# Output weights loaded between the two halves of a chunk's keys, and the keys of the last but one chunk in quarters

## The chip, the cores and the metric

One core of one Trainium2 chip runs the kernel; the rest of the chip is idle. The metric is device time in microseconds (us), the median of several executions.

## The reference, cut to what matters

Two decode attentions stand side by side. Part A has grouped heads and a window of 2048 positions; part B has 32 heads, 4 batches and the whole cache of 8192 positions. Part B is where the time is.

```
q = (x @ wq)                                # B = 4 rows, one token each
scores = einsum("bhqd,bhkd->bhqk", q, k_cache) * Dh ** -0.5     # 32 heads, Sk = 8192, Dh = 128
p = softmax(scores)
o = einsum("bhqk,bhkd->bhqd", p, v_cache)
out = o @ wo
```

Keys and values of part B are 537 MB of the 587 MB that have to be read, and each byte is used once. That is why loads are at the heart of it.

## The kernel before: the parts that matter

Part B is cut into 32 chunks (numbers 8 to 39) of 16 MB: four heads of one batch. A chunk has a stretch T on TensorE (PE), in which its keys are transposed and multiplied with q, then the statistics of the softmax, then the stretch PV with the values. Four chunks in a row (a group) share 512 KB of output weights, held in one buffer, `wos`. SyncE posts all big loads, in the order of the program, and waits before each until its buffer is free:

```
def dma_wos(hq):
    ...
    sch.add_dma("sp", <load B_wo of group hq into wos>, "d_wos",
                waits=[("reord", NCA + 4 * hq - 1)] if hq else [], ...)

for c in range(NCA, NC):            # NCA = 8, NC = 40
    if (c - NCA) % NB == 0:         # a new group
        dma_wos((c - NCA) // NB)
    dma_B("k", c)                   # two halves, 4 MB each; each waits for T of the half that it overwrites
    dma_B("v", c)                   # 8 MB; waits for PV of the chunk before
```

`reord` is the last PE instruction that reads the old output weights. It comes after all of T of the last chunk of a group. GpSimd relays the landings to PE: a first key half of a new group is called ready when both it and `wos` have landed.

The last chunks use smaller pieces, counted in tiles of 128 positions: keys of chunk 38 in `NEXTK = (64, 64, 128)`, values of 37 and 38 in `NEXTV = (128, 64, 64)`.

Of the kernel before, what the change touches and what calls it, by code (L numbers as in the profile page):

```python
# [13 lines left out]
TG = 8  # L14
# [6 lines left out]
SLAG = 2  # L21
NW = 64
LASTK = (32, 32, 64, 64, 64)
NEXTK = (64, 64, 128)
NEXTV = (128, 64, 64)
LASTV = (128, 64, 32, 16, 8, 8)
QK = (0, 4, 8, 16, 24)
QV = (0, 16, 24, 28, 30, 31)
# [140 lines left out]
def bass_concat_heads__sliding_block_cached__mha_block_cached__decode_kernel(  # L169
# [39 lines left out]
    NTA, NTB = chunks[0]["NT"], chunks[-1]["NT"]  # L209
    NONE = NC  # L210
    chunks.append(dict(chunks[NCA]))
    assert sum(LASTV) == sum(LASTK) == sum(NEXTK) == sum(NEXTV) == NTB and NTA * 16 == 1024 and NTB * 4 == 1024

    sch = _Sched()
    with ExitStack() as es:
        block = es.enter_context(nc.Block())

        def sb(name, shape, dt):
            return es.enter_context(nc.sbuf_tensor(name, shape, dt))
# [6 lines left out]
        wos = sb("wos", [P, 4, DO], BF16)  # L226
# [40 lines left out]
        semnames += ["d_h%d" % i for i in range(NH)] + ["d_bk0", "d_bk1", "d_bv0"]  # L267
        semnames += [f + str(i) for f, x in (("d_lk", LASTK), ("d_nk", NEXTK), ("d_lv", LASTV), ("d_nv", NEXTV)) for i in range(len(x))]
        semnames += ["d_wo%d" % i for i in range(NWO)] + ["d_wos"]
        sems = {n: es.enter_context(nc.semaphore(n)) for n in semnames}  # L270
# [43 lines left out]
        held = [[] for _ in range(NH)]  # L314
# [10 lines left out]
        def flat(at, n):  # L325
            return kv[:, at:at + n, :].rearrange("p s x -> p (s x)")
# [21 lines left out]
        def dma_wos(hq):  # L348


            src = B_wo[4 * hq * P:4 * (hq + 1) * P, :].rearrange("(p r) n -> p (r n)", r=4)
            sch.add_dma("sp", lambda e: e.dma_start(wos[:, :, :].rearrange("p r n -> p (r n)"), src), "d_wos",
                        waits=[("reord", NCA + 4 * hq - 1)] if hq else [], key=("wos", hq))
# [6 lines left out]
            src = T[:, ch["g"], SkA - W:, :].rearrange("b (pp j) d -> pp b (j d)", pp=P // NB)  # L360
            sch.add_dma("sp", lambda e: e.dma_start(kv[:, at, :], src), "d_h%d" % at, waits=waits, key=(kind, c))

        def dma_B(kind, c):


            ch = chunks[c]
            T, at, steps = (B_k, KB, QK) if kind == "k" else (B_v, VB, QV)
            src = T[ch["b"], 4 * ch["hq"]:4 * ch["hq"] + 4].rearrange("u (pp j) d -> (u pp) (j d)", pp=P // 4)
            dst = flat(at, 4)
            if kind == "k":  # L370
                pieces, fam = (LASTK, "d_lk") if c == NC - 1 else (NEXTK, "d_nk") if c == NC - 2 else ((NTB // 2,) * 2, "d_bk")
            else:
                pieces, fam = (LASTV, "d_lv") if c == NC - 1 else (NEXTV, "d_nv") if c in (NC - 2, NC - 3) else ((NTB,), "d_bv")
            j0, unit = 0, NTB // 4
            for i, n in enumerate(pieces):
                waits = []
                for u in range(j0 // unit, (j0 + n - 1) // unit + 1):
                    waits += held[at + u]
                x = slice(j0 * P, (j0 + n) * P)
                sch.add_dma("sp", lambda e, x=x: e.dma_start(dst[:, x], src[:, x]), fam + str(i), waits=waits, key=(kind, c, i))  # L380
                j0 += n
                sch.relay("pool", sems, "r_" + kind, n // TG, [(kind, c, i)] + ([("wos", ch["hq"])] if i == 0 and kind == "k" and ch["b"] == 0 else []))
            for g, end in zip(steps, steps[1:] + (NTB // TG,)):
                sch.tk[(kind + "r", c, g)] = ("r_" + kind, (c - NCA) * (NTB // TG) + end)
            for u in range(4):
                held[at + u] = [("T", ch["s"] + (u + 1) * unit // TG - 1) if kind == "k" else ("pv", c)]

        KB, VB = 0, 4

# [9 lines left out]
            dma_wo(c)  # L399
        for c in range(NCA, NC):  # L400
            if (c - NCA) % NB == 0:
                dma_wos((c - NCA) // NB)
            dma_B("k", c)
            dma_B("v", c)

        ms_read = []
# [495 lines left out]
```

## Time and profile before

| | before |
|---|---|
| median of the first three runs | 1386.8 us (1385.33 to 1389.99) |
| the profiled run | 1388.96 us, span 1387.2 us |
| DMA queue busy | 98.6% of 16 engines' span |
| PE busy | 89% |
| read from HBM | 587.21 MB, 423 GB/s over the span |

### The profile page before, as it was taken

The page shows a single profiled execution, that of the slowest core. Times are in us where ns is not written, and L with a number is a line of the kernel's source. Part 1 is how long each engine was busy: PE and PEld are TensorE (multiplying, and loading weights), DVE is VectorE, ACT ScalarE, POOL GpSimd, SP SyncE. Part 2 cuts the span into 40 slices and gives each one's busy share as a digit, 9 for nine tenths or more (in the row PEclk, how much of TensorE's full clock was granted, in tenths as well). Part 3 has the DMA queues.
Part 4 walks back from the last instruction along what each step waited for, and adds up shares of the span by engine and source line. Part 5 has one row for each costly group of instructions (what it writes and reads, how often), then busy time and mean ns, then how long its engine had stood idle before and what let it go on. Part 6 is the DMA issues. An engine that isn't in the chain of part 4 may idle for free.

```text
span 1387.2 us, 60816 instructions
## 1 busy us (share of the span) xinstructions
PE 1234.2 (89%) x27417; PEld 1137.9 (82%) x27417; DVE 744.6 (54%) x1335; ACT 513.9 (37%) x649; POOL 9.8 (1%) x29
## 2 busy tenths in 40 slices
PE   4898799989888989989898999989988889989998
PEld 4786788888887888888887888978888789878887
DVE  1675456655554556545554565545555555545555
ACT  1553244423333344333333443333333443333333
POOL 2000000000000000000000000000000000000000
PEclk9998999999999999999998899999999999999999
DMA  9999999899999999999999999999999999999997
GB/s 400 425 426 444 413 410 437 364 439 423 440 437 405 426 439 435 427 438 423 440 437 406 435 433 433 444 389 423 454 415 417 435 427 438 423 438 423 423 429 327
DMA packets 20652, 587.51 MB, mean 424 GB/s; under 512 B 2308, under 2 KB 2328, under 8 KB 4760
## 3 DMA queue, kind: packets, MB, share of 16 engines
q1 hardware_dynamic: 20600, 587.21, 98.6%
q8 instruction: 15, 0.25, 0.1%
q14 instruction: 5, 0.04, 0.0%
q10 hardware_dynamic: 32, 0.01, 0.0%
HBM read 587.21 MB, written 0.01 MB: 423 GB/s over the span
## 4 chain that ended last, share of the span: by engine, by line
DMA 55%; PE 41%; DVE 2%; issue 1%; ACT 1%; SPq 0%; POOLq 0%; DVEq 0%
DMA kv<-in_B_v_cache_dram 45%; PE po L414 20%; PE tr L412 12%; DMA kv<-in_B_k_cache_dram 8%; PE sc L414 6%; DMA kv<-in_B_wq_dram 2%; PE ms L414 1%; PE tr L414 1%; DMA kv<-in_A_k_cache_dram 1%; PE fin L414 1%; ACT pbb L594 1%; DVE kt L479 1%; DVE sA L532 0%; PE ms L412 0%; DVE gm L563 0%
## 5 line engine op out<-in xcount | busy, mean ns | idle before, releaser
L412 PE MATMUL tr<-identb,kv 128*128 128x128 bf16 x8704 | 666.7, 221 | 29.5 <-POOLq L72 23.3
L479 DVE COPY kt<-tr 128x1024 bf16<-128x1024 bf16 x736 | 501.9, 691 | 240.6 <-PE tr L412 238.0
L477 ACT ACTIVATE kt<-tr 128x1024 bf16<-128x1024 bf16 x352 | 359.6, 1024 | 730.8 <-PE tr L412 730.7
L412 PEld LDWEIGHTS tr<-identb,kv 128*128 128x128 bf16 x8704 | 508.9, 99 | 41.2 <-issue 31.0
L414 PE MATMUL sc<-qq,kt 128*128 128x64 bf16 x8192 | 398.0, 191 | 12.2 <-DVE kt L479 10.2
L414 PEld LDWEIGHTS po<-pbb,kv 128*128 128x128 bf16 x8192 | 306.2, 108 | 66.4 <-issue 56.4
L414 PE MATMUL po<-pbb,kv 128*128 128x64 bf16 x8192 | 309.8, 208 | 43.8 <-POOLq L72 39.6
L414 PEld LDWEIGHTS sc<-qq,kt 128*128 128x128 bf16 x8192 | 331.6, 98 | 15.7 <-DVE kt L479 13.1
L594 ACT ACTIVATE pbb<-sc,negb 32x128 bf16<-32x128 f32 x256 | 137.5, 537 | 123.2 <-DVE negb L577 120.1
L414 PE MATMUL tr<-wos,back 32*128 32x512 bf16 x512 | 80.5, 408 | 27.3 <-DVE kv L709 27.3
L661 DVE RECIPROCAL rinv<-ms 128x4 f32<-128x4 f32 (+1 forms) x40 | 7.8, 196 | 158.7 <-PE ms L414 158.7
L709 DVE CAST kv<-tr 128x512 bf16<-128x512 f32 x128 | 81.3, 683 | 12.3 <-PE tr L414 12.3
L599 DVE TENSOR_REDUCE rsb<-pbb 128x4 f32<-128x1024 bf16 x32 | 39.0, 1220 | 51.9 <-ACT pbb L594 51.9
L414 PEld LDWEIGHTS tr<-wos,back 32*128 32x128 bf16 x512 | 23.2, 96 | 49.1 <-DVE kv L709 30.1
L548 DVE TENSOR_REDUCE rh<-sc 128x4 f32<-128x512 f32 x64 | 43.9, 686 | 14.3 <-PE sc L414 14.3
L683 DVE TENSOR_TENSOR oz<-po,rz 128x16 bf16<-128x16 f32 x32 | 5.6, 175 | 67.9 <-PE po L414 67.9
L414 PE MATMUL sc<-qb,kt 128*128 128x64 bf16 (+3 forms) x512 | 26.4, 197 | 0.5 <-DVE gx L569 0.4
L414 PEld LDWEIGHTS ms<-gm,ind 4*128 4x128 f32 x64 | 9.4, 182 | 18.0 <-DVE gm L563 18.0
L414 PEld LDWEIGHTS sc<-qb,kt 128*128 128x128 bf16 x512 | 22.1, 102 | 2.4 <-issue 1.4
L414 PE MATMUL po<-pba,kv 128*128 128x64 bf16 x512 | 20.2, 198 | 3.1 <-issue 1.8
L414 PE MATMUL ms<-gm,ind 4*128 4x4 f32 x64 | 12.2, 258 | 11.9 <-DVE gm L563 11.9
L414 PEld LDWEIGHTS po<-pba,kv 128*128 128x128 bf16 x512 | 17.6, 101 | 5.1 <-ACT pba L616 4.2
(63 smaller groups left out, 210.7 us busy)
## 6 DMA issues: line engine op xcount, KB each, us to landing
kv<-in_B_k_cache_dram SPq DMA_DIRECT2D x61, 4096.0 KB, 26.4
kv<-in_A_k_cache_dram SPq DMA_DIRECT2D x8, 2048.0 KB, 13.3
kv<-in_A_v_cache_dram SPq DMA_DIRECT2D x8, 2048.0 KB, 14.6
kv<-in_B_v_cache_dram SPq DMA_DIRECT2D x3, 4096.0 KB, 21.4
kv<-in_B_v_cache_dram SPq DMA_DIRECT2D x5, 2048.0 KB, 27.5
kv<-in_B_k_cache_dram SPq DMA_DIRECT2D x5, 2048.0 KB, 28.4
kv<-in_A_wq_dram SPq DMA_DIRECT2D x1, 4096.0 KB, 12.5
kv<-in_B_wq_dram SPq DMA_DIRECT2D x1, 4096.0 KB, 27.1
```

The costliest lines, as they stand in the source:

```text
L412: sch.add("pe", lambda e: e.transpose(o, l, r), waits, key)
L414: sch.add("pe", lambda e: e.matmul(o, l, r, start=start, stop=stop), waits, key)
L477: sch.add("act", lambda e: e.activation(dst, src, ACTF.Copy), waits=waits, key=("ev", s))
L479: sch.add("dve", lambda e: e.tensor_copy(dst, src), waits=waits, key=("ev", s))
L548: sch.add("dve", lambda e: e.tensor_reduce(out=rh[:, half, :], in_=src, axis=AX.X, op=ALU.max), waits=[("S", ch["s"] + (half + 1) * ch["NG ...
L594: sch.add("act", lambda e, src=src, dst=dst, pp=pp, u=u: e.activation(dst, src, ACTF.Exp, bias=negb[pp, 0, u:u + 1], scale=scale), waits=[ ...
L599: sch.add("dve", lambda e: e.tensor_reduce(out=rst[1][:, :], in_=probs_of(c).rearrange("p j u -> p u j"), axis=AX.X, op=ALU.add), waits=[( ...
L661: sch.add("dve", lambda e: e.reciprocal(out=ri, in_=ms[:, L0:L0 + n]), waits=[("L", c)], key=("rinv", c))
L683: sch.add("dve", lambda e: e.tensor_tensor(out=o, in0=i0, in1=i1, op=ALU.mult), waits=waits, key=("oT", c))
L709: sch.add("dve", lambda e: e.tensor_copy(wol[:, u, :], o), waits=[("reord", c) if u == 3 else ("reord", c, u)] + [("fin", prev(c))], key=( ...
```

## The change

Its intent: the wait of the output weights should no longer hold up both halves of the next keys. The first half goes ahead of it. The diff, cut to its core (the rest lets one half be posted alone):

```
-NEXTK = (64, 64, 128)
-NEXTV = (128, 64, 64)
+NEXTK = (64, 64, 64, 64)
+NEXTV = (128, 64, 32, 32)
 ...
-    sch.relay("pool", sems, "r_" + kind, n // TG, [(kind, c, i)] + ([("wos", ch["hq"])] if i == 0 and kind == "k" and ch["b"] == 0 else []))
+    sch.relay("pool", sems, "r_" + kind, n // TG, [(kind, c, i)] + ([("wos", ch["hq"])] if i == 1 and kind == "k" and ch["b"] == 0 else []))
 ...
     if (c - NCA) % NB == 0:
+        dma_B("k", c, 0)
         dma_wos((c - NCA) // NB)
-    dma_B("k", c)
+        dma_B("k", c, 1)
+    else:
+        dma_B("k", c)
     dma_B("v", c)
```

More of the change, by code (lines that the diff above doesn't have):

```diff
@@ L361, in dma_A, with dma_B @@
             sch.add_dma("sp", lambda e: e.dma_start(kv[:, at, :], src), "d_h%d" % at, waits=waits, key=(kind, c))
-        def dma_B(kind, c):
+        def dma_B(kind, c, part=None):
             ch = chunks[c]
@@ L373, in dma_B @@
                 pieces, fam = (LASTV, "d_lv") if c == NC - 1 else (NEXTV, "d_nv") if c in (NC - 2, NC - 3) else ((NTB,), "d_bv")
-            j0, unit = 0, NTB // 4
+            j0, unit, used = 0, NTB // 4, {}
             for i, n in enumerate(pieces):
+                if part is not None and i != part:
+                    j0 += n
+                    continue
                 waits = []
@@ L378, in dma_B @@
                     waits += held[at + u]
+                    used[at + u] = [("T", ch["s"] + (u + 1) * unit // TG - 1) if kind == "k" else ("pv", c)]
                 x = slice(j0 * P, (j0 + n) * P)
@@ L381, in dma_B @@
                 j0 += n
-                sch.relay("pool", sems, "r_" + kind, n // TG, [(kind, c, i)] + ([("wos", ch["hq"])] if i == 0 and kind == "k" and ch["b"] == 0 else []))
+                sch.relay("pool", sems, "r_" + kind, n // TG, [(kind, c, i)] + ([("wos", ch["hq"])] if i == 1 and kind == "k" and ch["b"] == 0 else []))
             for g, end in zip(steps, steps[1:] + (NTB // TG,)):
                 sch.tk[(kind + "r", c, g)] = ("r_" + kind, (c - NCA) * (NTB // TG) + end)
-            for u in range(4):
-                held[at + u] = [("T", ch["s"] + (u + 1) * unit // TG - 1) if kind == "k" else ("pv", c)]
+            for u in used:
+                held[u] = used[u]
         KB, VB = 0, 4
```

## The prediction

> **What bounds the kernel now.** I read the page's busy shares first, then the chain of waits, the issue times of the DMA queue, and the DMA share in short windows. Names: c is a chunk, c = 0 to 7 in part A and 8 to 39 in part B; K0(c) and K1(c) are the two halves of its keys (4 MB each), V(c) its values (8 MB), wos the 512 KB of output weights that serve four chunks. T is the stretch of transposes and scores on PE, PV the stretch with the values.
>
> ```profile
> span 1387.2 us, 60816 instructions
> ...
> PE 1234.2 (89%) x27417; PEld 1137.9 (82%) x27417; DVE 744.6 (54%) x1335; ACT 513.9 (37%) x649; POOL 9.8 (1%) x29
> ...
> q1 hardware_dynamic: 20600, 587.21, 98.6%
> ...
> DMA 55%; PE 41%; DVE 2%; issue 1%; ACT 1%; SPq 0%; POOLq 0%; DVEq 0%
> ```
>
> PE at 89% looks like a candidate, but the DMA queue is busy 98.6% of the span. The chain in order of time says where each sets the pace:
>
> ```profile
> 284.75 31.96 DMA kv<-in_B_v_cache_dram
> ...
> 326.50 28.98 DMA kv<-in_B_v_cache_dram
> ...
> 364.71 29.55 DMA kv<-in_B_v_cache_dram
> ...
> 404.48 28.55 DMA kv<-in_B_v_cache_dram
> ...
> 442.70 31.62 DMA kv<-in_B_v_cache_dram
> ```
>
> Start plus duration is the landing of a V: 316.71, 355.48, 394.26, 433.03, 474.32. The steps are 38.77, 38.78, 38.77 and then 41.29. Inside a group of four chunks the step never leaves 38.8 by more than 0.5: that is 16 MB at full rate, and the DMA is the bound. Across a group boundary it is longer. Why, the DMA queue and short windows show at the first boundary (c = 11 to 12):
>
> ```profile
> 247.06 0.33 SPq L380 DMA_DIRECT2D kv<-in_B_v_cache_dram  x1
> 274.57 0.33 SPq L352 DMA_DIRECT2D wos<-in_B_wo_dram  x1
> 274.94 0.91 SPq L380 DMA_DIRECT2D kv<-in_B_k_cache_dram  x2
> 284.75 0.33 SPq L380 DMA_DIRECT2D kv<-in_B_v_cache_dram  x1
> 298.88 11.15 SPq L380 DMA_DIRECT2D kv<-in_B_k_cache_dram  x2
> ```
> ```profile
> 267.00:269.00 2.00, 2.00 (x52) 2.00 (x50) 1.33 (x3) 1.02 (x1) 0.00 (x0) 1.00 1.21 524
> 269.00:271.00 2.00, 1.70 (x30) 0.89 (x28) 1.37 (x3) 0.00 (x0) 0.00 (x0) 1.00 0.00 0
> 271.00:273.00 2.00, 0.78 (x4) 0.40 (x4) 1.31 (x4) 0.83 (x2) 0.00 (x0) 0.99 0.00 0
> 273.00:275.00 2.00, 2.00 (x14) 0.82 (x13) 1.34 (x3) 1.94 (x5) 0.00 (x0) 0.50 0.00 0
> 275.00:277.00 2.00, 2.00 (x42) 2.00 (x40) 0.68 (x2) 1.54 (x3) 0.00 (x0) 0.50 0.69 231
> ```
>
> The last two columns are DMA share and GB/s, counted where a packet starts (a window may read over 1 or 0 for that reason). No packet starts from 269 to 275. In an ordinary chunk (last line of the queue) K0 is posted when half of T is done and K1 11.15 us later. At a boundary nothing is posted between 247.06 and 274.57, because wos stands ahead of both and waits for the last reorder matmul of the chunk before, which comes after all of T. The table of the queue's waits has it: 7 waits, 189 us.
>
> ```profile
> SPq L352 <- PE tr L414: 189.0, 7, 27.3
> ```
>
> **What the Trainium skill says.** "DMA: Bandwidth & Descriptors", Anatomy of one DMA: DMA engines do not wait on semaphores; the issuing sequencer waits before it dispatches. So one blocked issue holds everything behind it, as the trace shows above. Same page, Queues, rings and completion order: on each engine descriptors are taken in ring order; a K0 posted early thus queues behind V and takes nothing from it. The trace agrees: K0 posted at 298.88 landed at 326.43, 9.72 after V. "HBM Reference", Specifications, gives about 425 GB/s for one core alone; the page here has a mean of 424, so there is no rate to be won, only idle time. "TensorE: Matmul & The Clock Gate", What's actually happening: PE falls to half clock after some 3.4 us of idleness. The windows show 0.50 near boundaries, so a PE that waits is slow just after; this shortens if the wait goes, and is no gain of its own while DMA is the bound.
>
> **The change part by part.** (1) K0 goes ahead of wos; wos then stands between K0 and K1, and the signal that K1 is ready, not K0, carries wos. No bytes and no compute instructions are added. Per boundary the cost now is the V-to-V step minus what a full queue would need: 38.78 for keys and values plus 1.22 for wos (512 KB loads behind other loads land 1.21 to 1.23 apart in part A). From the landings in the trace the seven steps are 45.28, 41.28, 40.51, 41.98, 41.35, 41.37 and 41.02: sum 292.79. Less 7 x 40.00 leaves 12.79 us: 5.28 at the first, 0.5 to 2.0 at each of the six others, where wos is posted only about 1 us ahead of V's landing, too late to start without a gap.
>
> Does the queue stay full afterwards? First boundary: T of c = 11 starts at 247.03, half of it is done after 10.9 us, so K0(12) is posted near 258, while V(11) moves until 271. K0 covers until 280.7. wos and K1 are posted at 274.6 to 275.4 as now, 5 us in hand. They last until 291.6, and V(12) is posted at 284.75. At the other boundaries the reorder ends about 1 us before V lands, so nearly all of K0's 9.7 us is in hand. So I take back all 12.79.
>
> (2) Keys of c = 38 in four quarters instead of 64, 64, 128. The chain at the end reads as if a load of 26.71 us set the pace, but the PE line shows what PE really waited:
>
> ```profile
> 1294.59 26.71 DMA kv<-in_B_k_cache_dram
> ```
> ```profile
> 1321.39 0.62 PE L412 MATMUL tr<-identb,kv 128*128 128x128 bf16 x8 [0.69 <-POOLq L72]
> ```
>
> T of c = 38 has run since 1309.5 on the first half; it stopped for 0.69 us before the big piece landed at 1321.29. In quarters the third lands some 4.85 earlier (1316.4), the fourth at 1321.4, when PE needs it only at about 1326. So 0.69 us is saved, not 4.85. From the landing of V(36) (1262.87) on PE is never idle longer than that: PV 9.5, then cycles of 36.7 (the PVs start at 1300.16, 1337.76, 1374.49). The end is a PE chain of 124 us hung on V(36); it moves with V(36) as a whole. Packets of half size cost the DMA, by the packet records, 9.78 instead of 9.70 us for the keys and 0.12 us for each of the two V tails. The last V landed at 1380.14 while PV ended at 1383.9, so this fits in the slack.
>
> (3) V tails of c = 37 and 38 in 32, 32 instead of 64: no gain. V(38) had landed at 1340.80, and PV needed its last quarter at 1344.4.
>
> Sum: 12.8 + 0.7 = 13.5 us. 1386.8 - 13.5 = 1373.3 us, a ratio of 0.990.
>
> **The rivals.** PE takes over as the bound. For: PV starts of c = 9 to 11 are 198.83, 236.66 and 274.54, steps of 37.8, only 1 us under the DMA's 38.78, and the chain there is PE's. With V(12) landing at 311.4, PE could start PV(12) only near 274.54 + 37.7 = 312.2: it gives back 0.8 at once. Against: the DMA doesn't starve from that (V(13) is posted at 322, K1(13) ends at 331), and PE regains 1 us per chunk. If the 0.8 stayed lost to the end, 1374.
>
> The wait moves to K1. If wos were released later than K0 ends, each boundary would run dry again. For: K1 is now posted about 5 us later than in an ordinary chunk. Against: the 5 to 9 us in hand worked out above. If half the gain were lost, 1380.
>
> The quarters give the full 4.85. For: the chain gives the big load 26.71 us. Against: the 0.69 of idle PE. It would be 1369.
>
> Nothing comes of it because the end is PE's: 1386. Against: the PE chain starts from a landing, and that moves.
>
> **Range and chances.** The runs of before spread from 1385.33 to 1389.99. With that and the rivals, 1370 to 1378 should hold it 8 times in 10. Two per cent faster would be 1359; all DMA idle time in the middle is 12.8, so this is out of reach: 0.02. Nothing is added that could cost 27 us: 0.01. Within 2%: 0.97.
>
> **What would show it.** Right: DMA share near 1 in every window from 247 to 1370; V-to-V steps at all seven boundaries near 40.0; V(36) landing near 1250; K0 at boundaries posted about half a T before wos; the 0.69 us wait of PE in c = 38 gone; PVs at the end still 36.7 apart. Wrong: windows of zero share behind a boundary's K0 (the wait moved to K1), V-to-V steps still above 41 at boundaries, or a chain that is PE's throughout part B.

## More of the kernel before

The page's second part cuts the span into 40 slices of 34.7 us. Its last row is what the DMA engines moved in each, in GB/s:

```profile
GB/s 400 425 426 444 413 410 437 364 439 423 440 437 405 426 439 435 427 438 423 440 437 406 435 433 433 444 389 423 454 415 417 435 427 438 423 438 423 423 429 327
```

Most slices are near 430. The eighth, 364, covers 243 to 277 us, where the first boundary between two groups of part B lies; slice 27 with 389 covers the boundary at 905 us. Such a row finds a hole quickly, but doesn't measure it: packets count where they start.

## The result, and the profile after

| | before | after |
|---|---|---|
| median | 1388.1 us (1385.33 to 1392.59, 6 runs) | 1374.87 us (1374.67 to 1377.15, 6 runs) |
| span of the profiled run | 1387.2 us | 1373.0 us |
| DMA queue busy | 98.6% | 99.5% |

The ratio is 0.9906, with a 95% interval of 0.9887 to 0.9925. Here and below a ratio is the mean time of one kernel's fast runs over that of the other's fast runs of the same rounds, so it isn't quite the ratio of the medians. The predicted ratio was 0.990, the predicted time 1373.3. All outputs are right.

Lines of the page of the changed kernel, for the ones that the prediction and the last section showed:

```profile
span 1373.0 us, 60822 instructions
...
GB/s 401 425 427 443 422 422 435 432 431 436 437 432 428 431 432 432 434 438 435 433 432 420 433 435 430 437 439 430 428 430 432 431 435 439 433 428 430 422 428 319
...
q1 hardware_dynamic: 21032, 587.21, 99.5%
...
DMA 52%; PE 43%; DVE 2%; ACT 1%; issue 1%; SPq 0%; POOLq 0%; ACTq 0%; DVEq 0%
```

Between the head and the last slice no slice is under 420. The issues of SyncE at the first boundary (start, duration, what) and the short windows there (PE, weight loads, DVE, ACT, GpSimd, then PE's clock, DMA share, GB/s):

```profile
243.38 0.33 SPq L384 DMA_DIRECT2D kv<-in_B_v_cache_dram  x1
254.27 0.33 SPq L384 DMA_DIRECT2D kv<-in_B_k_cache_dram  x1
270.98 0.33 SPq L352 DMA_DIRECT2D wos<-in_B_wo_dram  x1
271.35 0.43 SPq L384 DMA_DIRECT2D kv<-in_B_k_cache_dram  x1
280.87 0.33 SPq L384 DMA_DIRECT2D kv<-in_B_v_cache_dram  x1
```
```profile
269.00:271.00 2.00, 1.94 (x7) 0.55 (x8) 1.22 (x4) 1.95 (x4) 0.00 (x0) 0.50 1.03 442
271.00:273.00 2.00, 2.00 (x40) 2.00 (x40) 0.81 (x2) 1.80 (x4) 0.00 (x0) 0.50 0.99 426
273.00:275.00 2.00, 2.00 (x42) 2.00 (x40) 1.09 (x1) 0.00 (x0) 0.00 (x0) 0.50 0.95 410
```

The first half of the keys is now posted at 254.27, 10.89 us behind V. The output weights still wait until 270.98, but the DMA engines have the half to work on: a share of 1 where there was 0. The wait itself hasn't gone away, as the table of the queue's waits shows. It was 189.0 us before; what is left no longer holds up a load that the DMA engines run short of:

```profile
SPq L352 <- PE tr L421: 111.8, 7, 16.4
```

**Where the 14.26 us between the two profiled runs come from.** I followed the landings of V, as in the prediction. V of chunk 36 landed 14.24 us earlier (1262.87, then 1248.63); from there to the end both take the same, 124.37 and 124.33. The 14.24 split so: the seven boundary steps sum to 280.39 instead of 292.79 (each is now 40.05 or 40.06), which is 12.40. The 21 other steps sum to 1.50 less: 39.64, 39.01 and 39.22 at chunks 9, 17 and 22 became 38.8. V of chunk 8 landed 0.36 earlier. That is 14.26, the 0.02 too much being rounding. So 12.40 of it are where they were predicted. Two things were not: the 1.9 us away from the boundaries, and the tail, which gained nothing although it should have gained 0.7.

### The profile page after: what moved, and what is told of

It is laid out like the page before. It is cut to its first block, busy times and chain, and to the rows that moved or that the text cites. A ratio compares the mean times of both kernels' runs of the same rounds, so it can differ in the third digit from the quotient of the medians.

```text
span 1373.0 us, 60822 instructions
## 1 busy us (share of the span) xinstructions
PE 1229.9 (90%) x27417; PEld 1134.6 (83%) x27417; DVE 744.4 (54%) x1335; ACT 513.3 (37%) x649; POOL 9.8 (1%) x29
## 3 DMA queue, kind: packets, MB, share of 16 engines
q1 hardware_dynamic: 21032, 587.21, 99.5%
## 4 chain that ended last, share of the span: by engine, by line
DMA 52%; PE 43%; DVE 2%; ACT 1%; issue 1%; SPq 0%; POOLq 0%; ACTq 0%; DVEq 0%
DMA kv<-in_B_v_cache_dram 47%; PE po L421 22%; PE tr L419 12%; PE sc L421 6%; DMA kv<-in_B_k_cache_dram 2%; DMA kv<-in_B_wq_dram 2%; PE ms L421 1%; PE tr L421 1%; ACT pbb L601 1%; DMA kv<-in_A_k_cache_dram 1%; PE fin L421 1%; DVE sA L539 1%; DVE kt L486 1%; PE ms L419 0%; DVE gm L570 0%
## 6 DMA issues: line engine op xcount, KB each, us to landing
kv<-in_A_wq_dram SPq DMA_DIRECT2D x1, 4096.0 KB, 12.4
```

## The experiments

Theory A: the wait at the head of SyncE's queue emptied the DMA engines, and the gain is that idle time. Its rivals: B, that PE was sped up because first halves are now called ready without the output weights; C, that the quartered keys bring a large part; D, that it matters that the weights travel behind a half. All twelve kernels were timed in five rounds. For the first four the kernel before had a median of 1386.39 us, for the second four 1386.32, for the last four 1387.61.

| run | median us | ratio to before | 95% interval |
|---|---|---|---|
| move alone | 1376.12 | 0.9926 | 0.9912 to 0.9940 |
| pieces alone | 1385.45 | 0.9994 | 0.9977 to 1.0012 |
| weights posted by GpSimd | 1376.51 | 0.9926 | 0.9912 to 0.9940 |
| move, but not in the first group | 1376.92 | 0.9933 | 0.9919 to 0.9948 |
| first group alone | 1386.34 | 0.9996 | 0.9978 to 1.0014 |
| moved, but ready late | 1376.67 | 0.9931 | 0.9914 to 0.9947 |
| an eighth ahead | 1379.56 | 0.9952 | 0.9936 to 0.9968 |
| more loads in pieces | 1373.70 | 0.9908 | 0.9893 to 0.9922 |
| the changed kernel again | 1375.64 | 0.9916 | 0.9902 to 0.9929 |
| the move alone again | 1376.34 | 0.9919 | 0.9906 to 0.9931 |
| more loads in pieces again | 1374.81 | 0.9907 | 0.9893 to 0.9922 |
| weights behind both halves | 1376.80 | 0.9921 | 0.9907 to 0.9934 |

One thing holds for all variants that free half or all of the keys: the boundary steps came out as theory A expected, and where a gain in us was expected, it came out smaller. For the move alone 12.8 to 14 us were expected, for GpSimd's queue 12 to 13, for ready late about 12.4; the ratios give 9.6 to 11.2. The traces say why: V of chunk 36 landed at 1262.87, 1256.58 and 1258.11 in the three kept traces with the old order, 1259.2 in the mean, and at 1248.6 to 1249.5 in the eight that free half or all of the keys (those with more loads in pieces left out), 1248.9 in the mean. That is 10.3 us. The expectations had been taken from the first trace alone, the latest of the three.

### The move alone, and the pieces alone

```
# move alone: the changed kernel with
 NEXTK = (64, 64, 128);  NEXTV = (128, 64, 64)
# pieces alone: the kernel before with
 NEXTK = (64, 64, 64, 64);  NEXTV = (128, 64, 32, 32)
```

> Only the output weights move between the two key halves; keys of the last but one chunk and the value tails stay as before. Theory A (the blocked issue of the output weights emptied the DMA queue): the whole gain but for the last-chunk part, 12.8 to 14 us, ratio 0.990; the step from one landing of V to the next is 40.0 at all seven boundaries; PE's 0.69 us wait in chunk 38 is back. Theory C (the quartered keys bring a large part, up to 4.9 us): only 8 to 9 us, ratio 0.994.

> Only the quartered keys and the finer value tails; the output weights stand ahead of the keys as before. Theory A: 0.0 to 0.7 us, ratio 0.9995 to 1.000, V-to-V steps of 41 to 45 at the boundaries as before, PE's wait in chunk 38 gone. Theory C: 4 to 5 us, ratio 0.9965.

The move alone takes 1376.12 us, 10.3 us under before; the boundary steps in its trace are 40.05 to 40.08, and the wait of 0.69 us in chunk 38 is back, as expected. By its time alone it would not decide: 0.9926 lies between what A (0.990) and C (0.994) expected. The pieces alone do. They are not to be told from before, and the 0.9965 that C expected lies outside their interval. C falls.

The pieces-alone trace held a surprise. It has the old order, but its boundary steps sum to 286.77, not 292.79: the idle time there is 6.4 us over 7 x 40.06 and not 12.4. In the first step alone, 43.15 stands against 45.28. I come back to this below.

### The weights from another queue

```
-sch.add_dma("sp", lambda e: e.dma_start(wos[...], src), "d_wos", ...
+sch.add_dma("pool" if hq else "sp", lambda e: e.dma_start(wos[...], src), "d_wop" if hq else "d_wos", ...
-... if i == 0 and kind == "k" ...
+... if i == 1 and kind == "k" ...
```

> The output weights keep their place ahead of both key halves in time, but are posted by GpSimd instead of SyncE, so that their wait blocks nobody's keys; both key halves of a boundary are then posted at half and at all of T as in other chunks; the first group's stay on SyncE ahead of the keys. Theory A (it is the wait at the head of SyncE's queue that costs): V-to-V steps of 40.0 at the seven boundaries and 12 to 13 us gained, ratio 0.991. Rival D (the weights have to travel behind the first half, because they delay the keys): no more than half of it, ratio 0.995 or more, and steps above 40.5.

Issues of SyncE, and of GpSimd, at the first boundary of this kernel:

```profile
244.70 0.33 SPq L380 DMA_DIRECT2D kv<-in_B_v_cache_dram  x1
255.59 11.15 SPq L380 DMA_DIRECT2D kv<-in_B_k_cache_dram  x2
282.20 0.33 SPq L380 DMA_DIRECT2D kv<-in_B_v_cache_dram  x1
```
```profile
272.58 0.71 POOL L352 DMA_DIRECT2D wos<-in_B_wo_dram  x1 [261.14 <-PE tr L414]
```

Now a boundary looks to SyncE like any chunk: two halves whose issues start 10.82 us apart (the 11.15 of the merged line runs to the end of the second), with no wait of the weights between. The weights wait on another engine. GpSimd isn't idle, since it relays the landings in order, and at the six later boundaries the relay of V stood ahead of the weights there: they were posted only 0.58 us behind the landing of V, later than at the same six boundaries of before. That cost nothing either. The steps are 40.06 to 40.08, the time is that of the move alone, and D falls: it isn't the order of the bytes but whom the wait holds up.

### The readiness, and the place of the weights

```
# ready late: the move alone with
-... if i == 1 and kind == "k" ...
+... if i == 0 and kind == "k" ...
# weights behind both halves: the changed kernel with
 dma_B("k", c, 0)
-dma_wos((c - NCA) // NB)
 dma_B("k", c, 1)
+dma_wos((c - NCA) // NB)
```

> Posted in the order of the change, but the first key half of a boundary is declared ready only when the output weights have landed too, as before. Theory A (the gain is DMA time): steps of 40.05 at the seven boundaries, about 12.4 us gained; at most the 1.2 us of chunk 8 is lost. Rival B (the transposes of a boundary chunk started late, and PE is what was sped up): most of the gain is gone, under 6 us.

> The changed kernel with the output weights behind both halves of the keys, not between them. Theory A (only what stands posted ahead of the wait counts, and half of the keys already outlasts it): equal to the changed kernel, within 1 us, steps of 40.05 at the boundaries. If the second half was late in the changed kernel, this one is faster and its steps are shorter.

Ready late: 1376.67 us, steps 40.05 to 40.07. PE gets each first half later and it costs nothing that shows, so B falls. With the weights behind both halves the steps are 40.06 and 40.07 and V of chunk 36 lands at 1248.75, as in the changed kernel (1248.61). Its median is 1.2 us above the changed kernel's, a little more than the 1 us expected; the difference in the traces lies in the PE chain behind V of chunk 36 (126.2 against 124.9), which the edit doesn't touch. One half ahead is already enough.

### The first group of part B

```
# not in the first group: the move alone with, for chunk 8 only,
 dma_wos(0); dma_B("k", 8, 0); dma_B("k", 8, 1)      # as before, wos signalled with the first half
# first group alone: the kernel before with, for chunk 8 only,
 dma_B("k", 8, 0); dma_wos(0); dma_B("k", 8, 1)
```

> As the move alone, but the first group of part B (chunk 8) keeps its output weights ahead of the keys. In the changed kernel V of chunk 11 landed 1.2 us earlier than before, which the seven boundaries do not explain. If that is the order in chunk 8 (PE waited 1.40 us for its keys there), this kernel gains 1.2 us less than the move alone, about 12.4 us, and V of chunk 11 lands at 271.4 again; if it is only another run's scatter, the two are equal. The step at chunk 12 is 40.05 either way.

> Only chunk 8 has its output weights between the key halves; the seven boundaries are as before. Naive sum: 1.2 us gained. Theory A with PE as the clock of the release: PE, which is 3.6 us earlier at chunk 11 in the changed kernel while V lands only 1.2 earlier, releases the weights of chunk 12 earlier too, so the step there falls from 45.3 to about 42.9 and the gain is about 3.6 us, ratio 0.9974; the other six steps stay at 40.5 to 42.

I wanted an explanation for V of chunk 11, which landed 1.2 us earlier after the change, and looked for it in the order in chunk 8. Both expectations missed. Without the order in chunk 8 this V landed at 270.41, not at 271.4, and the time can't be told from the move alone. With it alone nothing is gained that can be seen (0.9996). The step at chunk 12 did come out as 43.12, near the 42.9 that I expected, but the pieces-alone kernel has 43.15 with the old order in chunk 8, so the hit proves nothing. Over all traces V of chunk 11 landed between 270.1 and 270.5 with the new order in chunk 8 and between 270.4 and 271.4 with the old. If the order does anything, it is about half a us. The profiled run of before was one with a late PE: its first PV of part B started at 160.47, in the 13 other traces between 155.7 and 159.6. Why, isn't known.

### How idle time depends on when the weights are posted

With three traces of the old order at the seven boundaries (before, pieces alone, first group alone) there are 21 boundaries. For each I took how late the output weights were posted against the landing of V, and how much the step was over 40.05:

| boundary | posted minus V landed, us | step minus 40.05, us |
|---|---|---|
| before, chunk 12 | +3.14 | 5.23 |
| first group alone, chunk 12 | +0.86 | 3.07 |
| before, chunk 32 | -0.74 | 1.32 |
| before, chunk 36 | -1.11 | 0.97 |
| before, chunk 20 | -2.03 | 0.46 |
| pieces alone, chunk 28 | -2.03 | -0.01 |

In all 21 the second number is at least the first plus 2.0; in 15 it is 2.0 to 2.6 more, in six 2.7 to 4.0. So the weights would have had to be posted 2.1 us ahead of the landing of V, and the old kernel managed at most 2.1. The packet records show most of these 2.1 us: at the first boundary of before the last packet of V ended 0.42 us ahead of the landing, and the first packet of the weights began 0.96 us after their issue did. That PE's lead ends at 2.1 fits its pace: in its faster cycle (the last of before) PE takes 36.73 us for a chunk, the DMA 38.78, so PE's release runs 2.05 ahead of V. When PE takes 37.6 us instead, the lead is 1.1 and a us is lost at the boundary. Which of the two it is goes with the clock. In the tails, where PE doesn't wait for keys, the clock records give 3.3 to 3.4 us at half clock in cycles of 36.7, 5.4 to 5.8 in cycles of 36.9, and 6.7 to 7.2 in cycles of 37.4 to 37.9. The old order sat on the edge, and the sum over the boundaries was 12.4, 8.9 and 6.4 us in three traces.

### A dose: one eighth of the keys ahead

```
# the kernel "not in the first group" with, at the seven boundaries,
+FIRSTK = (32, 96, 128)      # only the first 32 tiles, 1 MB, are posted ahead of wos
```

> A dose: at the seven boundaries only an eighth of the keys (32 of 256 tiles, 1 MB, 2.43 us of DMA) is posted ahead of the output weights, not half; chunk 8 as before. Theory A (gain = the shorter of what is posted ahead and the idle time): chunk 12 keeps 5.28 - 2.43 = 2.85 us, a step near 42.9; the other six, idle for 0.5 to 2.0, are covered, steps near 40.0 to 40.1; about 10 us gained in all, ratio 0.993. If it is only the order that counts, all steps are 40.05.

```profile
243.86 0.33 SPq L385 DMA_DIRECT2D kv<-in_B_v_cache_dram  x1
249.30 0.33 SPq L385 DMA_DIRECT2D kv<-in_B_k_cache_dram  x1
271.44 0.33 SPq L353 DMA_DIRECT2D wos<-in_B_wo_dram  x1
```
```profile
271.00:273.00 2.00, 2.00 (x33) 1.66 (x33) 0.69 (x1) 1.94 (x5) 0.00 (x0) 0.50 0.62 184
273.00:275.00 2.00, 2.00 (x42) 2.00 (x40) 1.22 (x1) 0.33 (x1) 0.00 (x0) 0.50 1.17 475
```

The step at chunk 12 is 40.28, not 42.9: in this trace the weights were posted only 0.54 us behind V's landing, so by the rule above 2.64 us had to be covered and 2.43 were. The share of 0.62 is the short hole. The 0.21 us left uncovered is close to the 0.22 over 40.06. The other steps are 40.12 to 40.40, about 0.1 of it from the smaller packets (32 tiles make 8 KB packets). So the dose works as theory A has it, but my size for chunk 12 was taken from the one late trace. The sum missed too: the ratio is 0.9952, some 7 us gained, where about 10 and 0.993 were expected. The median of 1379.56 is 3 us above the move alone, and the two traces differ by 2.7: 0.9 at the boundaries, 0.8 in other chunks, 1.1 in the tail. They were run at other times. Only the 0.9 is clearly the edit's; the rest stays open.

### The tail, and more loads in pieces

```
# more loads in pieces: the changed kernel with
-(NEXTK, "d_nk") if c == NC - 2 else ...
+(NEXTK, "d_nk") if c in (NC - 2, NC - 3) else ...
-(NEXTV, "d_nv") if c in (NC - 2, NC - 3) else ...
+(NEXTV, "d_nv") if c in (NC - 2, NC - 3, NC - 4) else ...
```

> The changed kernel with two more loads in pieces: V of chunk 36 as those of 37 and 38, keys of 37 in quarters as those of 38. If the end is a PE chain hung on V of chunk 36, PE can start its values at about 1245.9 instead of 1248.8 and go on without a wait: about 3 us faster than the changed kernel, 1371.7, with the last V landing as before at 1366.1 and PE ending right behind it. If the end is the DMA's, equal to the changed kernel.

> The changed kernel once more, beside the move alone and the two variants below on one chip. Expected 1374 to 1376 us, ratio 0.991; no 0.69 us wait of PE in chunk 38.

> The move alone, side by side with the changed kernel, whose two medians came from different chips' shares so far (1374.87 and 1376.12). Theory: the quarters are worth the 0.69 us wait, so this is 0.3 to 1.2 us slower than the changed kernel; the wait of 0.69 is there in its trace. If the clock phase of PE hides it, the two are equal.

> V of chunk 36 and keys of chunk 37 in pieces as well, side by side with the changed kernel: 1.2 us faster by the medians so far (1373.70 against 1374.87), expected 0.7 to 1.7 us faster again.

First the quarters. The big piece of keys of chunk 38 made PE wait in every trace with the old pieces in which PE kept its faster cycle (0.68 to 0.73 us in six traces). In the two others with the old pieces, an eighth ahead and the move alone again, PE's cycles were 37.6 and there was no such wait, although it was expected for the latter. In the kernel "not in the first group" and in the changed kernel run again, PE stands at the same place at the same time:

```profile
1306.28 0.40 PE L424 MATMUL sc<-qq,kt 128*128 128x64 bf16 x8
1307.40 0.62 PE L422 MATMUL tr<-identb,kv 128*128 128x128 bf16 x8 [0.73 <-POOLq L72]
```
```profile
1306.28 0.61 PE L419 MATMUL tr<-identb,kv 128*128 128x128 bf16 x8
1306.73 0.36 PE L421 MATMUL sc<-qq,kt 128*128 128x64 bf16 x8
1306.94 0.61 PE L419 MATMUL tr<-identb,kv 128*128 128x128 bf16 x8
```

The bracket is gone. Yet the tail of the profiled pair didn't get shorter. The last values stretch shows where it went, before and after:

```profile
1374.49 6.62 PE L414 MATMUL po<-pbb,kv 128*128 128x64 bf16 x168 [0.58 <-ACT pbb L594]
```
```profile
1359.60 7.23 PE L421 MATMUL po<-pbb,kv 128*128 128x64 bf16 x168
```

PE was ahead by 0.7 and then ran the first 168 matmuls 0.61 us slower. The clock records give half clock for 3.4 us in the first and 6.8 us in the second, from 1375.5 and from 1357.6. Windows there (the number ahead of the DMA share is the clock):

```profile
1376.00:1380.00 4.00, 4.00 (x97) 4.00 (x95) 1.22 (x1) 0.65 (x2) 0.00 (x0) 0.64 0.86 338
```
```profile
1357.10:1361.10 4.00, 3.31 (x33) 1.92 (x34) 2.52 (x5) 3.84 (x8) 0.00 (x0) 0.56 0.97 408
1361.10:1365.10 4.00, 4.00 (x91) 4.00 (x89) 1.22 (x1) 0.46 (x1) 0.00 (x0) 0.59 0.83 328
```

This falls one way or the other from run to run: from V of chunk 36 to the end the 12 traces other than the two with more pieces take 124.3 to 126.9 us. Side by side, the changed kernel is 0.70 us ahead of the move alone by the medians, which is the size of the wait, but also within the scatter of either (1374.35 to 1377.29, and 1375.55 to 1376.93). In the traces the gain gets as far as the PV of chunk 38: among those with the faster cycle it starts 74.04 and 74.24 us behind the landing of V of chunk 36 with the quarters, and 74.9 in all six without. That the quarters are worth 0.7 us at the end is therefore likely and not shown.

More loads in pieces have the lowest median: side by side 0.8 us ahead of the changed kernel by the medians and 1.1 by the means (1374.63 and 1375.78). The intervals against before overlap (0.9893 to 0.9922 and 0.9902 to 0.9929), so that it is faster than the changed kernel is likely and not shown. Expected were 3 us at first. PV of chunk 36 did start 2.7 us earlier (1246.14), but from there the PE cycles came out as 36.9, 37.9 and 38.3 in one trace and 37.6 three times in the other, where the changed kernel had 37.1, 36.7 and 36.9. The cycles of 37.9 and 37.6 hold 6.8 to 7.2 us at half clock, those of 36.7 some 3.4. The one of 38.3 is something else: PE, now earlier, ran into the DMA again and waited for a piece of the keys of chunk 39, which landed at 1337.31:

```profile
1337.41 0.62 PE L419 MATMUL tr<-identb,kv 128*128 128x128 bf16 x8 [0.85 <-POOLq L72]
```

So the next limit of the tail is the landing of those keys.

## Why the prediction was right, point by point

**DMA is the bound in the middle, and the boundary steps fall to 40.0.** Right. They are 40.05 to 40.08 in every kernel that frees half or all of the keys from the wait, whichever way it does it (but for the last step of the kernel with more loads in pieces, 40.28 and 40.29, where V of chunk 36 itself comes in small packets). The 0.05 is the weights' load, 1.27 us by the landings and not 1.22. That only idle time could be won also held, though the mean of 424 GB/s, which still has the idle time in it, isn't the rate of a full queue: 16.78 MB every 38.78 us are 433 GB/s, over the 425 that the prediction quotes.

**12.79 us at seven boundaries.** Right for the profiled pair (12.40), but it was read from one trace, and that trace was a high one. Two other traces of the old order had 8.9 and 6.4. The medians, from 10.3 us for the move alone to 13.2 for the whole change in its first call (12.0 in its second), say that the size was fair and somewhat high, and that the hit to 1.6 us was partly luck. The weakness of the step is that it took a number that depends on PE's clock phase for a property of the kernel.

**Enough keys in hand behind the wait.** Right. Posted 16.7 us ahead of the weights at the first boundary, the half lasted; a second half ahead of them brought nothing more.

**0.69 us for the quarters, not 4.85.** The wait of 0.69 us went, and the pieces alone brought nothing that 95% would tell from zero. The 4.85 is excluded. That the 0.69 would reach the end was not seen in the profiled pair.

**No gain from the finer value tails.** Nothing speaks against it: the pieces alone, which have them too, gain nothing that can be seen.

**PE as the next bound.** It was named as a rival with 0.8 us given back at once. Nothing of it can be seen: V of chunk 12 landed at 310.25 and its PV started at 310.44, and these 0.19 us are the same in the chunks after it (0.18 to 0.19). The V's landed 38.78 apart. PE had been earlier in this run: PV of chunk 11 started at 270.88 and not at 274.54.

**Lines that it misread.** None of these moved the sum. Inside a group the step did leave 38.8 by more than 0.5: it was 39.64 at chunk 9. The last PVs are not all 36.7 apart: 1300.16 to 1337.76 is 37.60, the wait of 0.69 included, and only the last step is 36.73. PE was idle for longer than 0.69 us in the tail, three times 0.85 us; it waited for DVE there, and no load is involved. And of the six later boundaries two had the weights posted 2.0 us ahead of the landing, not about 1. At the first boundary the half clock began at 272.9 and PE's longest gap ahead of it was 0.85 us, while the wait for keys of 3.14 us that ended at 287.86 had full clock behind it; the windows after the change show 0.50 too, and the clock records add up to 229 us at half clock before and 233 after.

**What was missed.** 1.5 us in chunks without a boundary (slow steps at 9, 17 and 22 in the profiled run of before) and 0.36 in chunk 8. I looked for a cause in chunk 8 and found none. More than half of the 1.5 is in chunk 9 and looks like the boundaries on a small scale: with PE late, V of chunk 9 was posted at 171.43, only 2.06 us ahead of the landing of the keys in front of it, and landed 20.39 behind them; after the change it was 4.19 ahead and took 19.35. No experiment varied this. Other traces with the old order at the boundaries are 0.6 and 1.2 us over the even pace in such chunks, so the rest may be scatter. It happens to stand against the 0.7 us that the tail didn't give, which is one reason why the sum fits so well.

What stays open: why six of the 21 boundaries lost 0.6 to 1.9 us more than their late posting explains. The packet records show where it was in the worst of them, chunk 24 of before: from 748.8 to 750.8, but for an instant, only 14 or 15 of the 16 DMA engines had a packet. That one late engine made the whole load late is likely and not shown, nor what held it up.

## What to carry to other kernels

When one engine posts all loads in order, look for the load whose wait ends latest and ask what stands behind it; put loads that are free to go ahead of it, or give the late one to an engine that has nothing to hold up. Where the DMA is the bound, as here with 98.6% busy, the gain of such a change is just the idle time, so measure it as the distance between landings less the time of the bytes, and over several traces, since it is a difference of two engines' paces. And a long wait in the chain isn't a saving: look at how long the waiting engine really stood.

## What the Trainium skill lacked or had wrong

- "DMA: Bandwidth & Descriptors", Latency and other measured facts, gives some 0.6 us to the first byte for a load posted by SyncE (here 0.63 us from the end of the issue to the first packet, for the weights at the first boundary of before); the fixed cost of about 2 us, in Anatomy of one DMA, is stated for GpSimd's path. What a kernel needs and no page has is how far ahead a SyncE load has to be posted for the engines not to run dry: here 2.0 to 2.6 us ahead of the landing of the load in front in 15 of 21 boundaries, and up to 4.0 in the others.
- "TensorE: Matmul & The Clock Gate" tells of gaps and of frequent short idles that lower the clock, and doesn't say how much idle time in a stretch is enough. Here the clock was halved for 3.4 or 6.8 us at a time in the tail, where PE's longest gap from PV of chunk 37 on was 0.86 us; the low stretches of the tails begin between 3.7 us ahead of the start of a PV and 1.0 behind it, so in or just behind the statistics, where short matmuls stand between waits. What it costs: PE's cycle is 36.7 us with some 3.4 us at half clock in it and about 37.6 with 6.9.
- No page gives the rate of one DMA engine by packet size over a range like this one's. The packet records show medians of 2.42, 1.21, 0.61, 0.31 and 0.16 us for 64, 32, 16, 8 and 4 KB, so 27 GB/s down to 26 GB/s: pieces with packets of 16 KB cost about 1%.
